# Decode step of gated attention and mixer MLP on one core: the prologue's weights loaded as w2, wq, w3, w4, with w3 in one load

## The chip, the core and the metric

One core of one Trainium2 chip runs the kernel. The metric is the device time of one execution in microseconds (us), the median of several runs. Engines are named as the profile names them: PE (matmul) with PEld (its weight loads), DVE (vector), ACT (scalar), POOL (GpSimd) and SP (which here only issues transfers). DMA stands for the 16 transfer engines of the core.

## What is computed

Two branches see the same two token rows (batch 2, width 1024) and are mixed by a gate. Branch A is one decode step of attention over caches of 16,384 keys and values for 32 heads of 128. Branch B is a shifted mixer with an MLP; with one token per row, each shift moves only zeros in.

```python
q = (x @ wq).reshape(B, 1, 32, 128)              # wq 1024 x 4096
p = softmax(q . k_cache * 128 ** -0.5)           # k_cache, v_cache: 2 x 32 x 16384 x 128, bf16
a = (p . v_cache) @ wo                           # wo 4096 x 1024
h  = gelu(layernorm(x) @ w1)                     # its four column groups are shifted along the sequence:
hs = concat(g0, g1, g2, g3) @ w2                 # with S = 1 all four are zero; w2 1024 x 1024
x1 = x + hs
b  = x1 + gelu(layernorm(x1) @ w3) @ w4          # w3 1024 x 3584, w4 3584 x 1024
g  = sigmoid(sum(x * gate_w))
out = g * a + (1 - g) * b
```

The caches are 2 x 268 MB and the weights that are read come to some 34 MB; each byte is read once.

## The kernel before

**The ring.** All large loads land in one SBUF tile, `ring`, of five slots; a slot holds 32 KB for each of the 128 partitions. The work on the caches is cut into 32 steps (`NPR`), each for two heads of one batch row. A step has one load of keys ("K", two slots, 64 KB for each partition, 8,192 KB in all) and one of values ("V", the same size). K loads use slots 2 and 3 in even steps and 3 and 4 in odd ones; V loads use slots 0 and 1.

**The weights.** They come ahead of the caches, through the same ring: wq (8,192 KB) in slots 0 and 1, w2 (2,048 KB) in slot 2, w3 (7,168 KB) in slots 3 and 4, and w4 (7,168 KB) in slots 0 and 1 again once wq has been used. Row r of a weight means the r-th of the rows that a partition holds: w3 has eight, of 7 KB each (3,584 numbers in bf16). In the kernel before, row 0 of w3 is a load of its own with the key `("w3", "first")`, and rows 1 to 7 are a second one (`runs(B_w3, F, 1, NBD - 1)`). Both land in the same slots and count on the same semaphore, `dr3`.

**What sets the order.** `queue_load` appends loads to a list, `pump` takes them off the front as soon as their slots are free in the program's order, and every one of them is issued by SP, in this order. Where a slot was used before, SP waits ahead of the issue for the PE matmul that read it last (`release`). A load at which SP waits holds up those behind it. The flag `more` lets the second load of w3 follow the first without asking for its slots. After the first load of the list SP adds 1 to a semaphore, `go`, for which ACT waits before it issues the small loads of x and gate_w (`xg_row`, L569 and L570). ACT's loads of `xrow` (L572) wait for POOL's constants.

**PE's prologue.** PE works in the order of the program: transposes of x (L590), q = x @ wq (256 matmuls, L605; the first waits for all of wq), a rearrangement of q (L614), the gate's sum (L401), the product with w2 (32 matmuls, L510), its columns (L550), layernorm's two sums (L401), the product with w3 (224 matmuls, L477, row by row: the first waits for all of w3) and the product with w4 (112 matmuls, L510 again). Then comes the loop over the 32 steps: DVE transposes the landed keys (L648), PE forms the scores (L654), a softmax follows, and PE takes the values (L690).

**What frees which slot.** The end of L605 frees slots 0 and 1 for w4. The end of w2's product frees slot 2, and the fifth of the eight rows of w3's product (140 of the 224 matmuls of L477) frees slot 3: K of step 0 waits for both. The end of w4's product frees slots 0 and 1 for V of step 0. After the loop the weights wo come in pieces of falling size into slots 2 and 3, and the output projection ends the kernel.

Of the kernel before, what the change touches and what calls it, by code (L numbers as in the profile page):

```python
# [120 lines left out]
def build_kernel(nc, A_x, A_k, A_v, A_wq, A_wo, B_w1, B_w2, B_w3, B_w4, gate_w, out, dbg=None):  # L121
# [3 lines left out]
    F = B_w3.shape[1]  # L125
# [13 lines left out]
    NBD = D // P  # L139
# [28 lines left out]
    with ExitStack() as st:  # L168
# [135 lines left out]
        def queue_load(key, fns, slots, more=False):  # L304
            dma_q.append((key, fns, slots, more))

        def pump():
            while dma_q and (dma_q[0][3] or all(i in slot_free for i in dma_q[0][2])):
                key, fns, slots, more = dma_q.pop(0)
                waits = () if more else sum((slot_free.pop(i) for i in slots), ())  # L310
                slot_of[key] = slots[0]
                slots_of[key] = slots
                for k, fn in enumerate(fns):
                    dsem = s_ring[slots[0]] if len(fns) == 1 else s_tail[k]
                    dma_done[key] = dma_done[key, k] = pl.dma("sp", (lambda e, fn=fn, idx=slots[0]: fn(e, idx)), dsem,
                                                              waits=waits if k == 0 else ())
                if key == ("w3", "first"):
                    pl.add("sp", lambda e: e.sem_inc(s_go, 1))

        def release(key, ev, slots=None):  # L320
            for idx in slots or slots_of[key]:
                assert idx not in slot_free
                slot_free[idx] = tuple(ev) if isinstance(ev, (tuple, list)) else (ev,)
            pump()
# [5 lines left out]
        def runs(Wt, width, r0, rn, base=0):  # L330
            def fn(e, idx):
                src = Wt.rearrange("(p r) n -> p (r n)", p=P)[:, r0 * width:(r0 + rn) * width]
                flat = ring[:, idx:, :].rearrange("p s m -> p (s m)")
                return e.dma_start(flat[:, (r0 - base) * width:(r0 - base + rn) * width], src)  # L334
            return fn
# [6 lines left out]

        wloads = {}
        wloads[("wq", 0)] = [runs(A_wq, HD, 0, NBD)]
        wloads[("w3", 0)] = [runs(B_w3, F, 1, NBD - 1)]
        wloads[("w4", 0)] = [runs(B_w4, D, 0, NBF)]
        for hi in range(2):
            wloads[("wo", hi)] = [runs(A_wo, D, r0, rn, hi * RS) if qn == NQ else cols_of(A_wo, D, r0, rn, q0 * DQ, qn * DQ, hi * RS)
# [3 lines left out]
        w_slots = {"wq": (0, 1), "w2": (2,), "w3": (3, 4), "w4": (0, 1)}  # L352
# [182 lines left out]
        w_order = []  # L535
# [21 lines left out]
        key = ("w2", 0)  # L557
        put([row_stage(key, list(range(NBD)), 0, NBD, lambda kc: shT_bf[:, kc, :], "const", last=True), hs_columns], key)
        put([st_x1, ln_a(x1T_f[:, :, :], "x1", st2_ps, "xn2"), ln_b(st2_ps, "xn2", None)])
        key = ("w3", 0)  # L560
        put([dense_stage(key, [kl], NBD, NBF, h3_ps, lambda kc: xn_bf[:, kc, :], "xn2", "h3", F) for kl in range(NBD)], key)
        put([gelu2])
        key = ("w4", 0)
# [7 lines left out]
        for qd in range(NQ):  # L571
            ev_xr = pl.dma("act", lambda e, qd=qd: e.dma_start(xrow[32 * qd:32 * qd + 2, :], A_x[:, 0, qd * DQ:(qd + 1) * DQ]), s_xr,  # L572
                           waits=(ev_xr0,))
        queue_load(("w3", "first"), [runs(B_w3, F, 0, 1)], w_slots["w3"])
        for key in [("wq", 0)] + w_order:
            queue_load(key, wloads[key], w_slots[key[0]], more=key[0] == "w3")
        for n in range(NPR):
            q_k(n)
            q_v(n)
        for pi in range(2):  # L580
            queue_load(("wo", pi), wloads[("wo", pi)], ((2, 3)[pi],))
        pump()

        def xcols(row, b_n, nb):
# [16 lines left out]
        key = ("wq", 0)  # L601
# [198 lines left out]
def bass_gated_mix__mha_block_cached__mixer_s_mlp__decode_kernel(  # L800
    nc: bass.Bass,
    A_x: bass.AP,
    A_k_cache: bass.AP,
    A_v_cache: bass.AP,
    A_wq: bass.AP,
    A_wo: bass.AP,
    B_x: bass.AP,
    B_w1: bass.AP,
    B_w2: bass.AP,
    B_w3: bass.AP,  # L810
    B_w4: bass.AP,
    gate_w: bass.AP,
    out: bass.AP,
):
    build_kernel(nc, A_x, A_k_cache, A_v_cache, A_wq, A_wo, B_w1, B_w2, B_w3, B_w4, gate_w, out)
# [28 lines left out]
```

## Time and profile before

| | |
|---|---|
| median of 3 runs | 1324.38 us (1324.28 to 1324.6) |
| the profiled execution | 1324.34 us |
| its span, first to last instruction | 1323.0 us |
| busy: PE, PEld, DVE, ACT, POOL | 794.4, 337.7, 659.9, 46.5, 23.5 us |
| transfers, MB | 570.60 in 11,114 packets |
| DMA busy share between 100 and 1280 us | 1.00 to 1.01 |
| granted PE clock, mean of the span | 0.78 |

The span is 1.34 us shorter than the execution's own time. In a row by windows the columns are the window, its length, the busy time of PE, PEld, DVE, ACT and POOL with the count of instructions that began in it, the granted PE clock, the busy share of the DMA engines and GB/s. A packet of a cache load is tens of KB and is put into the window in which it falls, so short windows can show over or under the sustained rate. In a timeline a merged row gives the start of its first instruction, the time in which they were busy or, on SP, the time from the first issue to the end of the last, and in brackets the idle time before. The time to landing of a load counts from its issue to its semaphore, with the time that it queued behind other loads.

### The profile page before, as it was taken

The numbers are of one execution on the slowest core, as the hardware profiler recorded it, in microseconds if no ns is written. First come the engines' busy times: TensorE is split into PE (matmuls) and PEld (weight loads), VectorE is DVE, ScalarE is ACT, GpSimd is POOL, SyncE is SP. The second block draws the span as 40 slices with busy tenths as digits, with TensorE's granted clock in tenths as the row PEclk, the third lists the DMA queues.
The fourth block names the chain that finished last, engine by engine and source line by source line (L and its number), as shares of the span: only waits on it lengthen the run. The fifth ranks groups of instructions, "written<-read, shape, count | busy, mean of one in ns | idle before, by whom it ended". The sixth has DMA issues, their size and how long they took to land.

```text
span 1323.0 us, 12314 instructions
## 1 busy us (share of the span) xinstructions
PE 794.4 (60%) x5235; PEld 337.7 (26%) x5235; DVE 659.9 (50%) x527; ACT 46.5 (4%) x101; POOL 23.5 (2%) x110
## 2 busy tenths in 40 slices
PE   1655567656556765655676565577565557756557
PEld 1622222212222222222222222222222222222223
DVE  0254446655444665544466554446655445665444
ACT  0000000000000000000000000000000000000000
POOL 3000000000000000000000000000000000000000
PEclk9977778786777877678787767878776787877678
DMA  9999999999999999999999999999999999999998
GB/s 417 433 423 435 436 432 432 436 432 440 428 434 438 428 434 438 430 434 436 430 438 432 430 438 432 430 440 430 430 440 430 430 440 430 430 440 430 430 440 367
DMA packets 11114, 570.60 MB, mean 431 GB/s; under 512 B 1232, under 2 KB 1756, under 8 KB 2015
## 3 DMA queue, kind: packets, MB, share of 16 engines
q1 hardware_dynamic: 11080, 570.43, 99.7%
q8 instruction: 8, 0.13, 0.0%
q14 instruction: 4, 0.02, 0.0%
q10 hardware_dynamic: 22, 0.01, 0.0%
HBM read 570.44 MB, written 0.00 MB: 431 GB/s over the span
## 4 chain that ended last, share of the span: by engine, by line
DMA 69%; PE 24%; DVE 6%; issue 1%; SPq 0%; POOL 0%
DMA ring<-in_A_k_cache_dram 65%; PE ps L654 23%; DVE ring L648 6%; DMA ring<-in_A_wo_dram 2%; DMA ring<-in_A_wq_dram 2%; PE ps L477 1%; PE ps L605 1%; DVE hsd L544 0%; PE ps L510 0%; PE ps L401 0%; SPq L334 0%; PE ps L729 0%; POOL mv L442 0%; DVE orow L763 0%; DVE q_f L617 0%
## 5 line engine op out<-in xcount | busy, mean ns | idle before, releaser
L654 PE MATMUL ps<-ring,Z 128*128 128x512 bf16 x2048 | 534.3, 420 | 375.9 <-DVE ring L648 374.6
L648 DVE STREAM_TRANSPOSE ring<-ring 128x2048 f32<-128x2048 f32 x256 | 565.2, 2274 | 264.6 <-DMA ring<-in_A_k_cache_dram 264.6
L654 PEld LDWEIGHTS ps<-ring,Z 128*128 128x128 bf16 x2048 | 204.2, 104 | 693.2 <-issue 459.3
L690 PE MATMUL ps<-ring,PT_sb 128*32 128x512 bf16 x2048 | 177.4, 523 | 4.3 <-DVE recip L681 3.9
L704 DVE SCALAR_TENSOR_TENSOR OT_sb<-ps,gT,recip 128x2 f32 x32 | 7.0, 220 | 213.0 <-PE ps L701 213.0
L690 PEld LDWEIGHTS ps<-ring,PT_sb 128*32 128x32 bf16 x2048 | 69.6, 126 | 98.4 <-issue 81.7
L675 ACT ACTIVATE P_sb<-ps,negm 128x512 bf16<-128x512 f32 x32 | 22.0, 687 | 995.5 <-DVE negm L673 995.5
L664 DVE TENSOR_REDUCE rA<-ps 128x1 f32<-128x512 f32 x32 | 22.1, 692 | 64.1 <-PE ps L654 64.1
L679 PE MATMUL ps<-rowsum,hsel 128*128 128x1 f32 x128 | 23.9, 291 | 38.0 <-ACT P_sb L675 38.0
L677 DVE STREAM_TRANSPOSE PT_sb<-P_sb 128x512 bf16<-128x512 bf16 x32 | 22.8, 711 | 27.1 <-ACT P_sb L675 27.1
L635 POOL TENSOR_TENSOR Z<-q_f,mask 128x8 bf16<-128x8 f32 x64 | 12.3, 227 | 1204.0 <-PE ps L654 1204.0
L679 PEld LDWEIGHTS ps<-rowsum,hsel 128*128 128x128 f32 x128 | 21.2, 235 | 40.7 <-ACT P_sb L675 40.7
L666 PE MATMUL ps<-ident,rmax_bf 128*1 128x128 bf16 x32 | 6.9, 217 | 33.1 <-DVE rmax_bf L665 33.1
L699 ACT ACTIVATE acc_sb<-ps 128x512 bf16<-128x512 f32 x32 | 19.1, 597 | 208.3 <-PE ps L690 208.3
L701 PE MATMUL ps<-dsel,acc_sb 128*128 128x2 bf16 x128 | 8.1, 167 | 22.5 <-ACT acc_sb L699 22.5
L605 PE MATMUL ps<-xT_bf,ring 128*128 128x2 bf16 x256 | 7.1, 165 | 18.4 <-DMA ring<-in_A_wq_dram 14.1
L477 PE MATMUL ps<-xn_bf,ring 128*128 128x2 bf16 x224 | 14.3, 202 | 1.4 <-DVE xn_bf L444 1.4
L701 PEld LDWEIGHTS ps<-dsel,acc_sb 128*128 128x128 bf16 x128 | 5.3, 96 | 38.3 <-ACT acc_sb L699 38.3
L666 PEld LDWEIGHTS ps<-ident,rmax_bf 128*1 128x1 bf16 x32 | 2.5, 79 | 48.9 <-DVE rmax_bf L665 48.9
L477 PEld LDWEIGHTS ps<-xn_bf,ring 128*128 128x128 bf16 x224 | 14.3, 162 | 1.4 <-issue 1.4
L667 DVE TENSOR_REDUCE m_sb<-ps 1x2 bf16<-1x128 bf16 x32 | 8.9, 279 | 9.9 <-PE ps L666 9.9
L673 DVE TENSOR_SCALAR negm<-ps,cAB 128x1 f32<-128x1 f32 x32 | 8.9, 277 | 9.2 <-PE ps L670 9.2
(99 smaller groups left out, 90.1 us busy)
## 6 DMA issues: line engine op xcount, KB each, us to landing
ring<-in_B_w_dram SPq DMA_DIRECT2D x1, 7168.0 KB, 26.4
ring<-in_B_w_dram SPq DMA_DIRECT2D x1, 6272.0 KB, 43.6
ring<-in_A_wo_dram SPq DMA_DIRECT2D x1, 4096.0 KB, 38.5
ring<-in_B_w_dram SPq DMA_DIRECT2D x1, 2048.0 KB, 28.1
ring<-in_A_wo_dram SPq DMA_DIRECT2D x1, 2048.0 KB, 22.7
ring<-in_A_wo_dram SPq DMA_DIRECT2D x1, 1024.0 KB, 24.8
ring<-in_B_w_dram SPq DMA_DIRECT2D x1, 896.0 KB, 4.6
ring<-in_A_k_cache_dram SPq DMA_DIRECT2D x32, 26.8
```

The costliest lines, as they stand in the source:

```text
L477: fn = lambda e, nb=nb, kl=kl: e.matmul(out_ps[:, nb, :], lhsT=cols(wv, kl, nb, nout), rhs=rhs_of(kl), start=False, stop=True, skip_group_ ...
L605: ev = pl.add("pe", lambda e, h=h, kc=kc: e.matmul(q_ps[:, h, :], lhsT=wv[:, kc, h * Dh:(h + 1) * Dh], rhs=xT_bf[:, kc, :], start=(kc == 0 ...
L635: ev = pl.add("pool", lambda e, hp=hp: e.tensor_tensor(Z[:, :, ZO:ZO + P].rearrange("p t (i c) -> p t i c", c=32)[:, :, 2 * hp:2 * hp + 2, ...
L648: return pl.add("dve", lambda e: e.transpose(ap, ap), waits=(arrived(("k", n)),), sig=True)
L654: ev = pl.add("pe", lambda e, bp=bp: e.matmul(S_ps[:, 0:NCOL], lhsT=Z[:, bp, ZO - 2 * u:ZO - 2 * u + P], rhs=kv[:, :, bp // 2, :, bp % 2], ...
L664: e1 = pl.add("dve", lambda e: e.tensor_reduce(rA[:, :], S_ps[:, 0:NCOL], axis=AX.X, op=ALU.max), waits=(ev_S[n],), sig=True)
L675: e7 = pl.add("act", lambda e: e.activation(P_sb[:, :], S_ps[:, 0:NCOL], ACT.Exp, bias=negm[:, 0:1], scale=scale, accum_out=rowsum[:, 0:1] ...
L677: e8 = pl.add("dve", lambda e: e.transpose(PT_sb[:, :], P_sb[:, :]), waits=(e7,), sig=True)
L679: e9 = pl.add("pe", lambda e, hp=hp: e.matmul(l_ps[:, hp:hp + 1], lhsT=hsel[:, hp, :], rhs=rowsum[:, 0:1], start=True, stop=True, skip_gro ...
L690: ev = pl.add("pe", lambda e, jj=jj, cg=cg: e.matmul(acc_ps[32 * cg:32 * cg + 32, 0:512], lhsT=PT_sb[:, 32 * jj:32 * jj + 32], rhs=vv[:, 4 ...
L699: e1 = pl.add("act", lambda e: e.activation(acc_sb[:, :], acc_ps[:, 0:512], ACT.Copy), waits=(ev_pv,), sig=True)
L701: e2 = pl.add("pe", lambda e, w=w: e.matmul(oT_ps, lhsT=acc_sb[:, w * P:(w + 1) * P], rhs=dsel[:, w, :], start=(w == 0), stop=(w == 3)), w ...
```

## The change

The list of weight loads becomes w2, wq, w3, w4. Row 0 of w3 is no longer loaded ahead of wq: w3 is one load of all eight rows, in third place. The signal `go` is given behind the first load of the list, which is now that of w2. `queue_load` is called without the flag `more`; the slots of w3 are free at that point, so it adds no wait.

```diff
-                if key == ("w3", "first"):
+                if key == ("w2", 0):
                     pl.add("sp", lambda e: e.sem_inc(s_go, 1))
...
-        wloads[("w3", 0)] = [runs(B_w3, F, 1, NBD - 1)]
+        wloads[("w3", 0)] = [runs(B_w3, F, 0, NBD)]
...
-        queue_load(("w3", "first"), [runs(B_w3, F, 0, 1)], w_slots["w3"])
-        for key in [("wq", 0)] + w_order:
-            queue_load(key, wloads[key], w_slots[key[0]], more=key[0] == "w3")
+        for key in w_order[:1] + [("wq", 0)] + w_order[1:]:
+            queue_load(key, wloads[key], w_slots[key[0]])
```

SP, the start of the program, before (-) and after (+). Each row is a load into the ring with the numbers for each partition (two bytes each); `e_pe` is a wait for PE.

```order
-L334 DMA ring<-in_B_w3_dram 128x3584
+L774 UNCONDITIONAL_BRANCH [waits barrier_Pool_Activation_PE_DVE_SP_release]
+L334 DMA ring<-in_B_w2_dram 128x8192
 L334 DMA ring<-in_A_wq_dram 128x32768
-L334 DMA ring<-in_B_w2_dram 128x8192
-L334 DMA ring<-in_B_w3_dram 128x25088
+L334 DMA ring<-in_B_w3_dram 128x28672
 L334 DMA ring<-in_B_w4_dram 128x28672 [waits e_pe]
 L361 DMA ring<-in_A_k_cache_dram 128x32768 [waits e_pe]
```

Ahead of wq there is now a load of 8,192 numbers for each partition instead of 3,584, and SP issues four weight loads instead of five. The numbers ahead of w4 are the same in sum (69,632), and w4 and K wait as before.

PE, the prologue behind the loads, before (`dr0`, `dr2` and `dr3` are the semaphores on which wq with w4, w2 and w3 land):

```order
L605 MATMUL ps<-xT_bf,ring 128x2 [waits e_dve,dr0]
L605 MATMUL ps<-xT_bf,ring 128x2 x255
L614 MATMUL ps<-q_sb,PermQ 128x64 [waits e_pool,e_dve]
L614 MATMUL ps<-q_sb,PermQ 128x64 x3
L401 MATMUL ps<-gin,ones_f 128x2 [waits e_dve]
L510 MATMUL ps<-ring,shT_bf 2x256 [waits dr2]
```

And after:

```order
L604 MATMUL ps<-xT_bf,ring 128x2 [waits e_dve,dr0]
L604 MATMUL ps<-xT_bf,ring 128x2 x255
L613 MATMUL ps<-q_sb,PermQ 128x64 [waits e_pool,e_dve]
L613 MATMUL ps<-q_sb,PermQ 128x64 x3
L401 MATMUL ps<-gin,ones_f 128x2 [waits e_dve]
L510 MATMUL ps<-ring,shT_bf 2x256 [waits dr2]
```

Nothing moved on PE: the product with w2 still stands behind that with wq, though w2 is now loaded first.

## The prediction

> **What bounds the kernel now.** I read the page's queue lines first, then the transfers by windows, then the chain of waits, and last the prologue in order of time, where the change lies.
>
> ```profile
> HBM read 570.44 MB, written 0.00 MB: 431 GB/s over the span
> 0.00:24.90 24.90, 0.62 (x8) 0.57 (x8) 2.64 (x11) 1.28 (x1) 10.53 (x45) 1.00 0.93 394
> 24.90:45.70 20.80, 11.17 (x306) 9.73 (x306) 5.08 (x17) 0.17 (x1) 0.00 (x0) 1.00 1.00 432
> 45.70:62.80 17.10, 14.61 (x226) 14.47 (x225) 1.30 (x7) 0.00 (x0) 1.06 (x3) 1.00 1.02 439
> 62.80:82.10 19.30, 5.80 (x112) 3.60 (x112) 3.16 (x10) 0.25 (x1) 0.00 (x0) 0.75 1.01 435
> 82.10:1280.00 1197.90, 733.18 (x4309) 296.99 (x4309) 626.18 (x465) 42.64 (x93) 11.89 (x62) 0.77 1.00 434
> ```
>
> The last two columns are the DMA engines' busy share and GB/s. From 24.9 us on the share is 1.00 to 1.02 and the rate 432 to 439 GB/s, in the rest of the prologue as in the loop. The 570.44 MB at the loop's 434 GB/s are 1314.4 us of the 1323.0 us span. What is left, 8.6 us, lies at the two ends. Ahead of 24.9 us the rate is 394 GB/s; those 24.9 us carry what 22.6 us would at 434, so 2.3 us are lost there, the first issue included.
>
> ```profile
> DMA ring<-in_A_k_cache_dram 65%; PE ps L654 23%; DVE ring L648 6%; DMA ring<-in_A_wo_dram 2%; DMA ring<-in_A_wq_dram 2%; PE ps L477 1%; PE ps L605 1%; DVE hsd L544 0%; PE ps L510 0%; PE ps L401 0%; SPq L334 0%; PE ps L729 0%; POOL mv L442 0
> ring<-in_B_w_dram SPq DMA_DIRECT2D x1, 7168.0 KB, 26.4
> ring<-in_B_w_dram SPq DMA_DIRECT2D x1, 6272.0 KB, 43.6
> ring<-in_B_w_dram SPq DMA_DIRECT2D x1, 2048.0 KB, 28.1
> ring<-in_B_w_dram SPq DMA_DIRECT2D x1, 896.0 KB, 4.6
> ring<-in_A_k_cache_dram SPq DMA_DIRECT2D x32, 26.8
> ring<-in_A_v_cache_dram SPq DMA_DIRECT2D x32, 29.2
> ```
>
> The chain gives 23% of the span to the score matmuls and 65% to the K loads. Read with the busy share it says less than it seems to: a load of keys is 8.39 MB, 19.3 us at 434 GB/s, and the median K load lands 26.8 us after its issue, a V load after 29.2. The difference of 7.5 and 9.9 us is mostly time in the queue behind the load before. PE's and DVE's work ahead of an issue runs while the DMA engines still empty that queue. So a moment saved or lost on PE changes the end only if it opens a hole in the stream. The row of 896 KB gives the part that is not queueing: 0.92 MB are 2.1 us at 434 GB/s, and this load, first of all and with nothing ahead of it, landed after 4.6. So 2.5 us go with issue, first data and signal; that is an upper figure for the lead at which a load must be issued if the stream is not to stop.
>
> **The prologue now.** The rows are of the timeline; behind them come the three waits of SP in the prologue (us in total, times, longest) and the queue of instructions (packets, MB, share of the engines).
>
> ```profile
> 0.74 0.40 SPq L334 DMA_DIRECT2D ring<-in_B_w_dram  x1
> 1.22 0.55 ACTq L569 DMA_DIRECT2D xg_row<-in_A_x_dram  x1
> 1.26 0.36 SPq L334 DMA_DIRECT2D ring<-in_A_wq_dram  x1
> 1.67 35.09 SPq L334 DMA_DIRECT2D ring<-in_B_w_dram  x3
> 10.22 0.62 PE L590 MATMUL ps<-ident,xg_row 3*128 3x3 bf16 x8 [10.22 <-DMA xg_row<-in_gate_w_dram]
> 16.01 0.17 DVE L594 COPY xT_bf<-ps 128x16 bf16<-128x16 bf16 x1
> 24.94 5.87 PE L605 MATMUL ps<-xT_bf,ring 128*128 128x2 bf16 x214 [14.10 <-DMA ring<-in_A_wq_dram]
> 35.15 1.26 PE L605 MATMUL ps<-xT_bf,ring 128*128 128x2 bf16 x42 [4.34 <-issue]
> 47.34 14.33 PE L477 MATMUL ps<-xn_bf,ring 128*128 128x2 bf16 x224 [1.35 <-DVE xn_bf L444]
> 56.38 0.33 SPq L361 DMA_DIRECT2D ring<-in_A_k_cache_dram  x1
> 63.77 5.80 PE L510 MATMUL ps<-ring,GT_bf 128*2 128x256 bf16 x112 [2.11 <-DVE GT_bf L462]
> 69.62 0.33 SPq L365 DMA_DIRECT2D ring<-in_A_v_cache_dram  x1
> 82.07 4.50 DVE L648 STREAM_TRANSPOSE ring<-ring 128x2048 f32<-128x2048 f32 x2 [9.62 <-DMA ring<-in_A_k_cache_dram]
> 94.15 0.33 SPq L361 DMA_DIRECT2D ring<-in_A_k_cache_dram  x1
> SPq L334 <- PE ps L605: 33.6, 1, 33.6
> SPq L361 <- PE ps L477: 19.6, 1, 19.6
> SPq L365 <- PE ps L510: 12.9, 1, 12.9
> q8 instruction: 8, 0.13, 0.0%
> ```
>
> SP issues four loads by about 2.5 us, waits 33.6 us for wq's matmuls and issues w4 near 36.4 (the end of 1.67 + 35.09 = 36.76, less an issue). w4 lands 26.4 us later, near 62.8. The second load of w3, issued near 2.1, lands near 45.7. PE starts with w3 only at 47.34, when DVE has normalized; so between wq's landing and the issue of K at 56.38 runs one unbroken chain that begins at 24.94 with wq.
>
> **The change, part by part.**
>
> *wq behind w2 instead of behind one row of w3.* By the listing of SP, 8,192 instead of 3,584 numbers for each partition precede wq: 4,608 x 2 bytes x 128 = 1.18 MB, 2.7 us at 434 GB/s. wq lands near 27.6 and the chain slips by 2.7 us: w4 is issued near 39.1, the product with w3 starts near 50.0, K is issued near 59.1, V near 72.3. On the path to the end this counts only where the queue ran dry, so I take the slack of each. w4: 7.34 MB are 16.9 us, it took 26.4, so 9.5 us over; less the lead of 2.5, 7.0 us of cover, 4.3 left after the slip. First K: 82.07 - 56.38 = 25.7 us less 19.3 leaves 6.4; less the lead, 3.9; after the slip 1.2 us left. First V: its data cannot start before K has landed at 82.07; issued at 72.3 it has 9.8 us, 7.3 with the lead taken off. From 82.07 on nothing remembers the slip: the second K needs the first to have landed and been used (94.15). Cost: 0. The cover is w3's transfer for w4 and w4's transfer for K.
>
> *The bytes ahead of w4 and K.* The four loads before w4 hold 69,632 numbers for each partition, the three after hold the same. w3 still ends near 45.7, w4 near 62.8, K at 82.1. Cost: 0.
>
> *w2 earlier.* It landed near 1.67 + 28.1 = 29.8; first in the stream it takes 0.7 + 4.8 + 2.5 = 8.0. Its only reader, the 32 matmuls of L510, stands on PE behind L605. Nothing starts sooner. Gain: 0.
>
> *One load fewer.* SP saves one issue, 0.36 to 0.40 us by the first two rows; SP then waits 33.6 us, so this is no gain. In the stream a hand-over from load to load falls away, and 7 KB rows become part of 56 KB rows. The trace has no price for that. The upper end is a gain of the 2.3 us lost ahead of 24.9, and most of those must go to the first issue at 0.74 and the first data, which stay. The lower end is 0: a loss is excluded as far as bytes go, since they are the same. It is nearest to the rows behind 24.9 us, where loads follow each other at 1.00 to 1.02: I take 0.05 us gained.
>
> *`go` behind the issue of w2.* ACT's loads of x start near 1.2 us as now. They shared the engines with wq's 64 KB rows and ended at 10.22; behind w2's 16 KB rows they can come earlier, and if they came twice as late, at 20, that would still be ahead of wq at 27.6. The readers wait until 16.01 for DVE, which follows POOL's constants. Cost: 0, under the cover of wq's transfer.
>
> *PE's gap.* In the middle of 256 like matmuls PE stood 4.34 us with nothing to wait for that the profile shows. It lies on the chain to K, so its size matters for the cover of 1.2 us. The change moves the transfers beside which it falls: w2's short rows and w3 before, w3 alone after. Bounds: 0, then K is issued earlier than now and nothing is gained; and twice, 8.7. The code and its count are the same, so I keep 4.3, between the ends. The Trainium skill bears on this gap: Runtime: NRT & Kernel Launch, Instruction fetch mechanics, says that the sequencer fetches the next 16 KB of instructions by DMA while it runs the current ones, and that crossing into them is mostly hidden. By that the gap would be gone, K's cover 5.5 us, the sum the same, and the slower rival below without its condition. The trace disagrees that it is hidden: 8 packets of instructions, 0.13 MB, went through these engines, and PE stood 4.3 us.
>
> Sum: 1324.34 - 0.05 = 1324.3 us by the profiled execution, of which 1323.0 are its span and 1.34 lie around it. That execution stands 0.04 us under the median of the three runs. Those spread over 0.32 us; a change below 0.2% (2.6 us) is what I call none.
>
> **Rivals.**
>
> *The merged load saves its fixed part (faster).* If each load paid its 2.5 us in series, one load fewer would give 1324.3 - 2.5 = 1321.8. For it: the 394 GB/s of the first window. Against: 64 cache loads follow each other at a busy share of 1.00, which leaves no room for 2.5 us each. The Trainium skill has this as a rule (DMA: Bandwidth & Descriptors, Anatomy of one DMA, a fit for loads issued by GpSimd): 2.0 us fixed for each load plus bytes over 436 GB/s; by it, in series, the time would be 1322.3. The trace agrees on a fixed part (2.5 us on the first load), and bears out no series.
>
> *K comes too late (slower).* Place: the issue of the first K at SP, behind PE's fifth row of w3. It decides once K slips by more than 3.9 us in all, 1.2 beyond the 2.7; beyond that each microsecond is a hole and costs one, as the whole stream moves. If PE's gap doubles (4.3 us more), the hole is 3.1 us: 1327.4, slower by 0.23%. w4 just keeps its cover (4.3 against 4.3). For it: the cover left is small and the gap is unexplained. Against: the lead of 2.5 us is an upper figure, since its last part, the signal, also lies in K's 25.7.
>
> *w2 early lets work start early.* It would need the product with w2 ahead of wq on PE, and the listing of PE shows the old order: no separate time.
>
> **How the numbers follow.** No hole and no fixed part, 1324.3: 0.87. Merged load or a shorter start worth something, 1321.8 to 1324.0: 0.06, of which 0.02 beyond 2.6 us. K or w4 late: 0.07, of which 0.05 beyond 2.6 us. So faster 0.02, same 0.93, slower 0.05. The range takes in the runs' spread, a gain of 1.1 of the 2.3 us in the first window and a hole of 1.9 us: 1323.2 to 1326.2.
>
> **What would show it.** The first PE matmul of L605 at 27.6 instead of 24.94; w4 issued near 39.1; w3's product from 50.0; K issued near 59.1 and landing in some 23 us instead of 25.7; DVE's first transpose still at 82.1 within 0.5; the busy share at 1.00 from 27 us on. I am wrong if the first transpose comes later by more than 1 us (a hole; then the share of 60 to 65 us shows it), or earlier by more than 1 us (a fixed part).

## The result, and the profile after

The changed kernel takes 1326.47 us, median of 22 runs, between 1324.44 and 1327.6; the kernel before 1324.37 us, median of 22, between 1324.12 and 1324.63. The ratio is 1.0014, 95% interval 1.0008 to 1.0021: slower by 2.1 us, and that by less than the 0.2% that I called none, but clear of noise and above the top of my range (1326.2). The kernel before repeats within 0.5 us, the changed one spreads over 3.2: four of its 22 runs lie at 1324.4 to 1324.6, as fast as before, and 18 between 1325.7 and 1327.6. So one profile does not tell of this kernel. The first that was taken, of 1324.44 us, is one of the four. Its loop in the transfers by windows:

```profile
82.10:1280.00 1197.90, 732.93 (x4309) 296.19 (x4309) 626.09 (x465) 42.61 (x93) 11.89 (x62) 0.77 1.00 433
```

And its prologue in order of time (L604 is q's matmul, L647 DVE's transpose of the keys, one line up from before):

```profile
8.37 0.63 PE L589 MATMUL ps<-ident,xg_row 3*128 3x3 bf16 x8 [8.37 <-DMA xg_row<-in_gate_w_dram]
28.09 5.87 PE L604 MATMUL ps<-xT_bf,ring 128*128 128x2 bf16 x214 [19.10 <-DMA ring<-in_A_wq_dram]
35.74 1.26 PE L604 MATMUL ps<-xT_bf,ring 128*128 128x2 bf16 x42 [1.78 <-issue]
56.98 0.33 SPq L361 DMA_DIRECT2D ring<-in_A_k_cache_dram  x1
82.37 17.66 DVE L647 STREAM_TRANSPOSE ring<-ring 128x2048 f32<-128x2048 f32 x8 [10.47 <-DMA ring<-in_A_k_cache_dram]
```

The loop streams as before (433 against 434 GB/s). wq's first matmul comes 3.15 us later than before, but PE's gap in the middle of q's matmuls is 1.78 us instead of 4.34, so the first K is issued only 0.6 us later, and lands as before (82.37 against 82.07). Two more profiles of the same kernel are of executions of 1326.76 and 1326.54 us. The prologue of the first of them in order of time:

```profile
28.25 5.86 PE L604 MATMUL ps<-xT_bf,ring 128*128 128x2 bf16 x214 [19.22 <-DMA ring<-in_A_wq_dram]
37.93 1.26 PE L604 MATMUL ps<-xT_bf,ring 128*128 128x2 bf16 x42 [3.82 <-issue]
59.17 0.33 SPq L361 DMA_DIRECT2D ring<-in_A_k_cache_dram  x1
84.45 17.66 DVE L647 STREAM_TRANSPOSE ring<-ring 128x2048 f32<-128x2048 f32 x8 [9.24 <-DMA ring<-in_A_k_cache_dram]
123.11 17.66 DVE L647 STREAM_TRANSPOSE ring<-ring 128x2048 f32<-128x2048 f32 x8 [10.14 <-DMA ring<-in_A_k_cache_dram]
```

Here the gap is 3.82 us, the first K is issued at 59.17 and is in use at 84.45, 2.4 us later than before; the second follows 38.66 us on, at the loop's own pace. 1326.76 - 1324.34 is 2.4 us too. The whole loss of this execution is in the landing of the first K. The transfers between 62 and 64 us, in the kernel before:

```profile
62.00:64.00 2.00, 0.23 (x8) 0.19 (x12) 1.18 (x6) 0.25 (x1) 0.00 (x0) 1.00 1.13 492
```

And in this execution, where they move 262 GB/s instead of 492:

```profile
62.00:64.00 2.00, 2.00 (x34) 2.00 (x34) 0.00 (x0) 0.00 (x0) 0.00 (x0) 1.00 0.76 262
```

### The profile page after: what moved, and what is told of

It reads as the page before. It is cut to its first block, busy times and chain, and to the rows that moved or that the text cites. A ratio compares the mean times of both kernels' runs of the same rounds, so it can differ in the third digit from the quotient of the medians.

```text
span 1323.1 us, 12297 instructions
## 1 busy us (share of the span) xinstructions
PE 793.9 (60%) x5235; PEld 337.4 (26%) x5235; DVE 659.7 (50%) x527; ACT 46.4 (4%) x101; POOL 23.5 (2%) x110
## 4 chain that ended last, share of the span: by engine, by line
DMA 69%; PE 24%; DVE 6%; issue 1%; SPq 0%; POOL 0%
DMA ring<-in_A_k_cache_dram 65%; PE ps L653 22%; DVE ring L647 6%; DMA ring<-in_A_wq_dram 2%; DMA ring<-in_A_wo_dram 2%; PE ps L477 1%; PE ps L604 1%; DVE hsd L544 0%; PE ps L510 0%; PE ps L401 0%; SPq L334 0%; SPq L340 0%; POOL mv L442 0%; DVE orow L762 0%; DVE q_f L616 0%
## 5 line engine op out<-in xcount | busy, mean ns | idle before, releaser
L647 DVE STREAM_TRANSPOSE ring<-ring 128x2048 f32<-128x2048 f32 x256 | 565.2, 2275 | 262.1 <-DMA ring<-in_A_k_cache_dram 262.1
L689 PE MATMUL ps<-ring,PT_sb 128*32 128x512 bf16 x2048 | 180.9, 531 | 4.6 <-DVE recip L680 4.6
L604 PE MATMUL ps<-xT_bf,ring 128*128 128x2 bf16 x256 | 7.1, 165 | 20.9 <-DMA ring<-in_A_wq_dram 19.1
```

Source lines behind the costliest of these rows:

```text
L604: ev = pl.add("pe", lambda e, h=h, kc=kc: e.matmul(q_ps[:, h, :], lhsT=wv[:, kc, h * Dh:(h + 1) * Dh], rhs=xT_bf[:, kc, :], start=(kc == 0 ...
L647: return pl.add("dve", lambda e: e.transpose(ap, ap), waits=(arrived(("k", n)),), sig=True)
L689: ev = pl.add("pe", lambda e, jj=jj, cg=cg: e.matmul(acc_ps[32 * cg:32 * cg + 32, 0:512], lhsT=PT_sb[:, 32 * jj:32 * jj + 32], rhs=vv[:, 4 ...
```

## The experiments

The theory was that the first K is issued too late for the stream to go on behind w4 ("late K"); the rivals were the one load of w3, the order of the loads as such, and something in the stream itself.

**The changed kernel again** (no edit).

> The changed kernel once more, for a second profile and more times, since its runs lie between 1324.4 and 1327.6 us and the one profiled execution is at the fast end. Theory 'late K': the longer executions are those in which PE's gap inside q's matmuls (L604; 1.78 us in the first profile of this kernel, 4.34 before) is longer, so that the first K is issued after 59 us and the stream has a hole near 61 to 64 us; a profile of 1326 us or more shows a gap of 6 to 8 us and DVE's first transpose 2 to 3 us after 82.1; a profile of 1324.5 shows a gap under 4 us. Rival 'the stream itself': the longer executions have the first K issued before 59 us and lose time elsewhere, in the rate of the loop or at the end.

Measured: 1326.19 us, median of 11, between 1324.38 and 1327.45; ratio 1.0012 (1.0003 to 1.0021). The profile, of 1324.70 us, had a gap of 1.68 us and the first K at 57.24. It fits the theory's short case and could not show the long one. (The long executions profiled later have a gap of 3.8 us, not the 6 to 8 that I expected.)

**wq first again, w3 still one load.**

```diff
-                if key == ("w2", 0):
+                if key == ("wq", 0):
...
-        for key in w_order[:1] + [("wq", 0)] + w_order[1:]:
+        for key in [("wq", 0)] + w_order:
```

> Undoes one part: wq is again the first large load, ahead of w2; w3 stays one load, and no row of it comes ahead. wq lands near 22.8 us, 2.1 us sooner than in the kernel before. Theory 'late K': the cover is larger than before, so 1324.3 us within 0.3 with a spread of some 0.5 us. Rival 'the one load of w3 costs' (its 56 KB rows or the missing hand-over): as slow as the change, 1326 to 1327 us and spread out.

Measured: 1324.33 us, median of 11, between 1324.14 and 1324.48; ratio 0.9999 (0.999 to 1.0008).

```profile
22.96 5.87 PE L604 MATMUL ps<-xT_bf,ring 128*128 128x2 bf16 x214 [7.09 <-DMA ring<-in_A_wq_dram]
46.05 14.35 PE L477 MATMUL ps<-xn_bf,ring 128*128 128x2 bf16 x224 [3.51 <-DMA ring<-in_B_w_dram]
55.12 0.33 SPq L361 DMA_DIRECT2D ring<-in_A_k_cache_dram  x1
82.32 17.67 DVE L647 STREAM_TRANSPOSE ring<-ring 128x2048 f32<-128x2048 f32 x8 [11.00 <-DMA ring<-in_A_k_cache_dram]
```

With wq at 22.96 the product with w3 waits for w3 itself, K is issued at 55.12, and no run is longer than before. The one load of w3 costs nothing, and gains nothing: one load fewer than before, and the same time.

**w2 ahead of wq, w3 in two loads.**

```diff
-        wloads[("w3", 0)] = [runs(B_w3, F, 0, NBD)]
+        wloads[("w3", 0)] = [runs(B_w3, F, 1, NBD - 1)]
...
+            if key == ("w3", 0):
+                queue_load(("w3", "first"), [runs(B_w3, F, 0, 1)], w_slots["w3"])
-            queue_load(key, wloads[key], w_slots[key[0]])
+            queue_load(key, wloads[key], w_slots[key[0]], more=key[0] == "w3")
```

> The other part alone: w2, wq, then w3 in two loads as before (row 0, then rows 1 to 7), both behind wq. Theory 'late K': wq lands as late as in the changed kernel (28 us), so the same times, 1326.5 us median, between 1324.4 and 1327.6. Rival 'the one load of w3 costs': 1324.3 us.

Measured: 1325.9 us, median of 11, between 1324.62 and 1326.73; ratio 1.001 (1.0001 to 1.0019). So w2 ahead of wq is the part that costs. The profile, of 1326.73 us, shows wq in use at 28.20, a gap of 3.35 us, the first K issued late, and a second loss:

```profile
58.66 0.33 SPq L361 DMA_DIRECT2D ring<-in_A_k_cache_dram  x1
82.75 17.66 DVE L649 STREAM_TRANSPOSE ring<-ring 128x2048 f32<-128x2048 f32 x8 [8.01 <-DMA ring<-in_A_k_cache_dram]
121.68 17.66 DVE L649 STREAM_TRANSPOSE ring<-ring 128x2048 f32<-128x2048 f32 x8 [9.06 <-DMA ring<-in_A_k_cache_dram]
161.69 17.66 DVE L649 STREAM_TRANSPOSE ring<-ring 128x2048 f32<-128x2048 f32 x8 [11.52 <-DMA ring<-in_A_k_cache_dram]
```

The first K is 0.7 us late against the kernel before, the third comes 40.0 us after the second where 38.7 is the pace. The theory names the first loss alone; the second is taken up below, where the prediction is judged.

**More PE instructions ahead of wq's.**

```diff
-        for nb in range(NBD):
+        for nb in list(range(NBD)) * 13:
             last = pl.add("pe", lambda e, nb=nb: e.transpose(
```

> The changed order of loads, with 96 more PE transposes of x ahead of wq's matmuls (the eight of L589 thirteen times over, into the same place, while PE waits for wq anyway), so that PE's instructions reach their next block before wq has landed. Theory 'late K by a gap in which PE waits for its instructions': no gap inside wq's matmuls, they end near 28.1 + 7.1 = 35.2 us, K is issued near 55.2 and the time is 1324.3 us within 0.3, in all runs. Rival 'the slip by wq alone': K stays late in some runs, 1325 to 1327 us. Rival 'the stream itself': no difference from the changed kernel, 1326 to 1327 us.

Measured: 1326.02 us, median of 11, between 1325.37 and 1326.37; ratio 1.0012 (1.0003 to 1.0021). A miss, since the edit did not do what it was for; the time is what both rivals gave, so this run says nothing against them.

```profile
28.99 6.72 PE L604 MATMUL ps<-xT_bf,ring 128*128 128x2 bf16 x246 [14.20 <-DMA ring<-in_A_wq_dram]
37.91 0.40 PE L604 MATMUL ps<-xT_bf,ring 128*128 128x2 bf16 x10 [2.20 <-issue]
58.29 0.33 SPq L361 DMA_DIRECT2D ring<-in_A_k_cache_dram  x1
82.52 17.66 DVE L647 STREAM_TRANSPOSE ring<-ring 128x2048 f32<-128x2048 f32 x8 [9.35 <-DMA ring<-in_A_k_cache_dram]
121.21 17.66 DVE L647 STREAM_TRANSPOSE ring<-ring 128x2048 f32<-128x2048 f32 x8 [8.48 <-DMA ring<-in_A_k_cache_dram]
161.45 17.66 DVE L647 STREAM_TRANSPOSE ring<-ring 128x2048 f32<-128x2048 f32 x8 [8.82 <-DMA ring<-in_A_k_cache_dram]
q8 instruction: 9, 0.15, 0.0%
```

The gap did not go: it moved, from behind matmul 214 to behind matmul 246, and took 2.20 us. With 96 more ahead, 246 is 128 matmuls further on in PE's program than 214 was, and the page of this run counts nine packets of instructions (the row `q8`) where every other one counts eight. That fits a wait for instructions at places 128 matmuls apart: one of them was passed while PE waited for wq, and the next one still lies among wq's matmuls. K went out at 58.29, and most of the loss, 1.5 us, again lies between the second and the third K (40.2 us).

**The slip without the loads.** The kernel before, with DVE's work between w2's product and its columns done two and three times.

```diff
-            for ps, sl in ((rows_ps, slice(0, P // 2)), (rows2_ps, slice(P // 2, P))):
+            e1 = None
+            for ps, sl in ((rows_ps, slice(0, P // 2)), (rows2_ps, slice(P // 2, P))) * 2:      # 3 in the second
...
-                    waits=(evd["rows"], ev_const), sig=True)
+                    waits=(evd["rows"], ev_const, e1), sig=True)
```

> The kernel before, its loads untouched, with DVE's two multiplications of L544 done twice (the second time into the same place with the same values): 2.5 us more in the chain from wq to the first K, behind w4's issue, and not one load or PE instruction more. First K issued near 58.9. Theory 'late K': the same times as the changed kernel, some at 1324.4 and some 1 to 3 us more, median 1325 to 1326.5. Rival 'two instruction blocks or small loads fall on one DMA engine, because the loads stand in another order': 1324.3 us, all runs within 0.5.

Measured: 1324.48 us, median of 11; eight runs between 1324.22 and 1324.62, three between 1326.21 and 1326.46; ratio 1.0005 (0.9995 to 1.0014). The kernel before, run beside it, took 1324.17 to 1324.67 us in 32 of 33 runs and 1325.22 in one. The median is below what I expected. The profile, of 1324.62 us, had a gap of 2.06 us and the first K at 56.96, only 0.6 us later than in the kernel before with its gap of 4.34; the short gap took up most of the slip.

> The same with L544 done three times over: 4.9 us more in the chain. First K issued near 61.3, when the first DMA engines have ended w4. Theory 'late K': every run has a hole of 1.5 to 3 us, 1326 to 1328 us. Rival 'order of loads': 1324.3 us.

Measured: 1326.09 us, median of 11, between 1324.9 and 1327.33; ratio 1.0013 (1.0004 to 1.0022). Four runs, of 1324.9 to 1325.3 us, lie below the 1326 that I expected of all.

```profile
33.27 1.26 PE L606 MATMUL ps<-xT_bf,ring 128*128 128x2 bf16 x42 [2.56 <-issue]
59.54 0.33 SPq L361 DMA_DIRECT2D ring<-in_A_k_cache_dram  x1
83.71 17.67 DVE L649 STREAM_TRANSPOSE ring<-ring 128x2048 f32<-128x2048 f32 x8 [8.09 <-DMA ring<-in_A_k_cache_dram]
```

With every load where it was, DVE's work that takes 5 us longer in the chain costs 1.7 us. That falls to the late K alone; the order of the loads is not needed for it.

**The changed kernel with the same slip added.** The first edit of the two above, in the changed kernel.

> The changed kernel with L544's multiplications done twice: 2.5 us more behind w4's issue. First K issued at 59.5 us or later. Theory 'late K': no run at 1324.4 any more; 1326 to 1329 us, and the profile shows DVE's first transpose at 83 us or later. Rival 'order of loads': as the changed kernel, 1324.4 to 1327.5 us.

Measured: 1326.93 us, median of 11, between 1326.48 and 1327.55; ratio 1.0019 (1.001 to 1.0028). No run near 1324.4 is left. The profile, of 1327.18 us, shows the hole at its widest. The transfers between 60 and 62 us in the kernel before:

```profile
60.00:62.00 2.00, 1.67 (x27) 1.58 (x25) 0.26 (x2) 0.00 (x0) 0.00 (x0) 1.00 1.23 520
```

The same window in this kernel:

```profile
60.00:62.00 2.00, 2.00 (x35) 2.00 (x34) 0.00 (x0) 0.00 (x0) 0.00 (x0) 1.00 0.20 86
```

And its first K in order of time:

```profile
61.75 0.33 SPq L361 DMA_DIRECT2D ring<-in_A_k_cache_dram  x1
84.72 17.66 DVE L648 STREAM_TRANSPOSE ring<-ring 128x2048 f32<-128x2048 f32 x8 [6.90 <-DMA ring<-in_A_k_cache_dram]
```

There the DMA engines are busy for 0.20 of the time instead of 1.23 and move 86 GB/s. K lands 23.0 us after its issue; nearly all of w4 was through by then, so of this 3.7 us are not transfer (19.3).

**w2's product ahead of wq's on PE**, with the loads as in the changed kernel.

```diff
+        ev_q4 = ev_r0
+        for run in pro_stages[:6]:
+            run()
         q_ps = banks[1][:, 0:H * 2].rearrange("p (h b) -> p h b", b=2)
...
-        q4_ps = banks[2][:, 0:NBP * G].rearrange("p (t g) -> p t g", t=NBP)
+        q4_ps = banks[6][:, 0:NBP * G].rearrange("p (t g) -> p t g", t=NBP)
...
-        for run in pro_stages:
+        for run in pro_stages[6:]:
```

> The changed order of loads with PE's order made to fit: the gate, the product with w2, its columns and layernorm stand ahead of q = x @ wq (q's rearrangement moves to another PSUM bank for it). The chain from wq to the first K loses the 10 us between wq's last matmul and w3's product, which then waits for w3 near 46; K is issued near 55. Theory 'late K': 1324.3 us in all runs, within 0.5, and first K lands by 82.4. Rival 'order of loads': 1324.4 to 1327.5 us, as the changed kernel.

Measured: 1324.63 us, median of 11, between 1324.54 and 1324.77; ratio 1.0002 (0.9993 to 1.0011).

```profile
35.97 2.51 PE L608 MATMUL ps<-xT_bf,ring 128*128 128x2 bf16 x88 [3.05 <-issue]
46.17 14.36 PE L477 MATMUL ps<-xn_bf,ring 128*128 128x2 bf16 x224 [6.97 <-DMA ring<-in_B_w_dram]
55.23 0.33 SPq L361 DMA_DIRECT2D ring<-in_A_k_cache_dram  x1
```

wq is as late as in the changed kernel and the gap is there, but neither lies on the way to K any more: PE waits 6.97 us for w3. The spread is gone. The early w2 has a use if its reader is early too; it buys no time, since the stream is the bound.

**The first K in two halves**, in the changed kernel.

```diff
+                if key == ("k", 0):
+                    slots = k_slots[0]
...
+        def k0_half(h):
+            return lambda e, idx: e.dma_start(ring[:, 2 + h, :], kv_src(A_k, 0)[:, h * SLOT:(h + 1) * SLOT])
...
-            q_k(n)
+            if n == 0:
+                queue_load(("k", "a"), [k0_half(0)], (2,))
+                queue_load(("k", 0), [k0_half(1)], (3,))
+            else:
+                q_k(n)
```

> The changed kernel with the first K loaded in two halves of 4,096 KB: the one into slot 2, which w2's product has freed by 42 us, is issued behind w4, the one into slot 3 where the whole K was issued. PE's chain stays as late as in the changed kernel (second half issued at 57 to 59.5 us), but the stream has 9.7 us of work behind w4. Theory 'late K by a hole behind w4': 1324.3 to 1324.7 us in all runs, first transpose by 82.5. Rival 'something else in the late chain, w4 or V, costs the time': 1324.4 to 1327.5 us as the changed kernel.

Measured: 1324.7 us, median of 11, between 1324.51 and 1325.0; ratio 1.0003 (0.9994 to 1.0012). Five runs lie above the 1324.7 that I gave as the end, by 0.3 us at most.

```profile
37.68 1.26 PE L613 MATMUL ps<-xT_bf,ring 128*128 128x2 bf16 x42 [3.78 <-issue]
43.09 16.14 SPq L579 DMA_DIRECT2D ring<-in_A_k_cache_dram  x2
82.43 17.66 DVE L656 STREAM_TRANSPOSE ring<-ring 128x2048 f32<-128x2048 f32 x8 [7.93 <-DMA ring<-in_A_k_cache_dram]
```

This execution (1324.51 us) has the long gap, 3.78 us, and issues the second half near 58.9 (the end of 43.09 + 16.14 less an issue), as late as the long executions issue the whole K. With the first half in the queue since 43.09 there is no hole: 82.43. So w4, V and the rest of the late chain cost some 0.3 us at most, by the medians (1324.7 against 1324.37 for the kernel before); a first K that is not there when w4 ends costs the rest.

**Three more profiles of the changed kernel** (no edit).

> The changed kernel, one more look for a profile of a longer execution. Theory 'late K', with the bounds that the runs so far give: first K issued by 57.3 us gives 1324.4 to 1324.7; from 58.3 us on the first transpose comes after 82.5 and the execution takes 1325.4 us or more, at 61.7 near 1327.2. PE's gap in L604 is then 3 us or more. Rival: a longer execution with the first K issued before 57.5 us and the first transpose by 82.5.

> As the look before it: the time follows the issue of the first K, and through it PE's gap in L604.

> As the look before it: the time follows the issue of the first K, and through it PE's gap in L604.

Measured: 1326.76, 1324.51 and 1326.54 us. The first stands in the section on the result. In the second the gap is 2.21 us, K goes out at 57.27 and is used at 82.37; in the third 3.81, 59.22 and 84.14. All profiles with one load for the first K, in the order of its issue:

| kernel | gap, us | first K issued | first transpose | execution, us |
|---|---|---|---|---|
| wq first | 2.87 | 55.12 | 82.32 | 1324.41 |
| w2's product early | 3.05 | 55.23 | 82.44 | 1324.59 |
| before | 4.34 | 56.38 | 82.07 | 1324.34 |
| before, L544 twice | 2.06 | 56.96 | 82.56 | 1324.62 |
| changed, first profile | 1.78 | 56.98 | 82.37 | 1324.44 |
| changed, second profile | 1.68 | 57.24 | 82.42 | 1324.70 |
| changed, fourth profile | 2.21 | 57.27 | 82.37 | 1324.51 |
| changed, more PE | 2.20 | 58.29 | 82.52 | 1326.37 |
| w3 in two | 3.35 | 58.66 | 82.75 | 1326.73 |
| changed, third profile | 3.82 | 59.17 | 84.45 | 1326.76 |
| changed, fifth profile | 3.81 | 59.22 | 84.14 | 1326.54 |
| before, L544 three times | 2.56 | 59.54 | 83.71 | 1326.09 |
| changed, L544 twice | 4.10 | 61.75 | 84.72 | 1327.18 |

Up to 57.27 every execution is within 0.4 us of the kernel before; from 58.29 on each is 1.7 us or more above it. No version was faster than the kernel before; wq first is its equal with one load fewer.

## Why the prediction was wrong

The mechanism that happened stands in the prediction as a rival, "K comes too late", with its place. I gave it 0.07 and let it begin only once K slips by more than 3.9 us in all. The step that failed is the cover of the first K, 1.2 us after the slip. In two executions of the changed kernel K went out at 59.17 and 59.22, just where I had it (59.1), and the 1.2 us were not there: the first transpose came at 84.45 and 84.14 instead of 82.1. The three terms of the cover, measured:

- *The lead, 2.5 us, called an upper figure.* This is the term that was mis-sized. A first K issued at 57.27 kept the stream whole, one at 58.29 did not; w4 lands near 62.8 (the profile before). So the lead, counted to w4's landing as my sum counts it, is between 4.5 and 5.5 us. I took it from the landing of the very first load, into idle engines and 7 KB for each partition; the K that found the queue almost empty took 3.7 us beside its transfer, in 64 KB rows. And a load lands when its last part is there, while its engines end one by one. The traces hold a record of each packet (start, length, size), which none of the views above lists; put in rows, each packet behind the one whose end it meets, they make sixteen, one for each engine. The first engine ends w4 at 60.4 to 60.7 us in all 13 profiles of the table, the last at 62.2 to 62.8. Counted to the first, the K at 57.27 is 3.3 us early and the one at 58.29 is 2.4. So a lead of 2.5 us was nearly right for the first engine; what the sum left out is the two us between the first engine and the last. (The first V was read in the same way: its data starts at 79.86 us in the kernel before, when the first engine ends K, and not after 82.07. There it cost nothing.)
- *The slip, 2.7 us.* wq's first matmul came at 27.95 to 28.47 in the five profiles, 3.0 to 3.5 after 24.94.
- *The gap, 4.3 us, kept.* It was 1.68, 1.78, 2.21, 3.81 and 3.82: not a constant, and in the profiles of the changed kernel this decides between short and long executions. With the gap of before the changed kernel would issue K near 56.38 + 3.3 = 59.7, with a short one it stays under 57.3.

With a lead of 5 and a slip of 3.3 the kernel before has 6.4 - 5 = 1.4 us of cover and the changed one, at the same gap, 1.9 too little: 4.3 - 1.9, so a gap below some 2.4 us is needed. The three profiles with a gap of 2.21 or less are those near 1324.5: they reach the forecast time by a short gap that I had not foreseen, which is luck.

The price was wrong too. I had one microsecond of hole for each of lateness. By the first transpose against the 82.07 of before, measured are 0.5 and 0.7 us with K at 58.3 and 58.7, 2.1 and 2.4 at 59.2, 1.6 at 59.5 and 2.65 at 61.75: steep, then flat. By the packet records the engines do not lose the same. From 46 to 90 us they are idle for less than 0.1 us on average with K at 58.29 and 58.66, for 0.55 and 0.33 at 59.17 and 59.22, for 0.13 at 59.54 and for 1.6 at 61.75; in addition some of the first packets of a late K take up to 4.4 us instead of 2.42, and others none of that. Every engine carries eight packets of each cache load, and a load lands with its slowest engine, so the time follows the engine that lost most. Why the first packets of a late K take so long stays open.

The second loss of 1.3 to 1.5 us, between the second and the third K, stands in two of the six profiles with a K from 58.29 on and in none of the seven with a K by 57.27. The records give it a cause. Between 147 and 150 us a packet of instructions holds up one engine by 1.5 us, in the kernel before too; there it meets an engine that had ended the load before 1.6 us ahead of the last one, and nothing is lost. In "more PE" and "w3 in two" it meets an engine that the late K had put at the end or within 0.2 us of it, and that engine then lands the third K alone, at 160.96 and 161.21 us instead of 159.00.

Right were: the same bytes ahead of w4, nothing gained by an early w2 while its reader stands behind wq (its median is above, not below), nothing gained by one load fewer (wq first: 1324.33 against 1324.34 for the kernel before on the same chip), so the rival of the merged load fell; `go` behind the issue of w2 cost nothing (x in use at 8.37 instead of 10.22); and from the third K on the loop keeps its pace (38.7 us a step in every profile). The fixed 2.0 us for each load (the Trainium skill, DMA: Bandwidth & Descriptors, Anatomy of one DMA, a fit for loads issued by GpSimd) are not paid in series by these loads of SP: wq first, with one load fewer, shows no gain. The rule of the Trainium skill on instruction blocks (Runtime: NRT & Kernel Launch, Instruction fetch mechanics: mostly hidden) would have given the changed kernel its cover; the trace disagrees, with 1.7 to 4.3 us in each of the 14 profiles.

## What to carry to other kernels

When a stream is the bound, write down for each load how long before the end of the load ahead it is issued, and compare that with the smallest such distance that a run has shown to be enough, not with the fixed part of an isolated load: here 5.5 us were enough and 4.5 were not, since the first of the sixteen engines was through with the load ahead some two us before it landed. A change that moves no bytes can still spend that reserve, and then the time spreads before it rises; the spread of the runs against that of the kernel before is the first sign. What helped here was to take the late chain off the issue (a smaller piece that can go out early, or the reader moved to where its data now lies) or to start the chain as early as before (wq first).

## What the runs showed of the hardware that was not expected

PE's gap in a run of like matmuls sits at a fixed count of instructions: behind PE's 222nd matmul in 13 profiles (wq's 214th, or its 168th with w2's product and layernorm ahead), and behind its 350th, 128 further on, with 96 transposes more ahead. In each of the 14 profiles the packet records have a packet of instructions of 16,384 bytes that ends 1.2 to 1.5 us before PE goes on: in the kernel before it runs from 32.67 to 33.63 us, PE stands from 30.80 and goes on at 35.15; in the short first profile of the changed kernel from 33.50 to 34.48, PE stands from 33.96 to 35.74. So PE waits there for its next instructions, and its gap, 1.7 to 4.3 us, varies with the moment at which that packet is carried by DMA engines that are full. What decides this moment stays open. The kernel before has the gap too; there it is invisible in the time, as the cover of K takes it up.

The sixteen engines end one load between 60.4 and 62.8 us, and what one engine loses, to a late load or to a packet of instructions, the others do not make up for: the 1.5 us between 147 and 150 us cost nothing where they met an engine with time to spare, and 1.4 to 1.7 us where they met one of the last (by the second-last engine's end, 159.30 and 159.85).
